# Attention with routed experts on one core: the merge of late batches, the gate and the first score are put at other places of a hand-written order

## The chip, the core and the metric

The kernel runs on one core of a Trainium2 chip. The metric is the device time of one execution in microseconds; three executions of the kernel before took 556.55 to 557.47 us, with a median of 557.07 us. The names of engines are those of the profile: PE is TensorE (matrix products, and transposes as products with an identity), PEld its weight loads, DVE is VectorE, ACT is ScalarE, POOL is GpSimd, SP is SyncE, which here only issues transfers.

## The reference

```python
batch, n_heads, seq, head_dim = (8, 12, 448, 64)
q_n, k_n = (rmsnorm(q, g_q), rmsnorm(k, g_k))
scores = scale * np.matmul(q_n, k_n.transpose(0, 1, 3, 2))
attn = softmax(scores)
x = matmul(attn, v)                 # as [3584 tokens, 768]
...
logits = x @ w_gate                 # 8 experts, w_gate [768, 8]
expert_idx = argmax(logits); gate_w = softmax(logits)[expert_idx]
for e in range(8):
    tok_idx = the tokens of expert e, at most the 80 with the largest gate_w
    h = maximum(x[tok_idx] @ w1[e], 0)      # [768, 1024]
    out[tok_idx] = gate_w[tok_idx] * (h @ w2[e])
```

So the attention of all 8 batches has to be done before it is known which 80 tokens each expert takes.

## The kernel before, in words

**Attention.** The 8 batches of 12 heads are cut into 24 groups `g` of 4 heads, three to a batch. A group has 7 rounds: six tiles of 128 keys (2 pairs of heads by 3) and one round with the 64 keys that are left of all four heads. A round is a score (L302: PE writes two banks of PSUM, ACT takes the exponential into an `at` tile) and, later, the product with V (`av`, L323). `presum` (L346, on DVE) adds the `at` tiles of a pair of heads, and `zl` (L366, on PE) brings those sums and the product of the attention output with the gate's weights into one bank. Ahead of its first score a group needs `square` (ACT), `rstd` (DVE; a power on POOL), `normalise` (POOL; DVE for the first two groups) and four `transp` (L281): (a, u) with a = 0 for q and 1 for k, and u for the pair of heads. Each `transp` is three or four PE transposes into the one bank `tp`, which ACT copies into `qkT`.

**Order.** Nothing is scheduled by a planner: the loop at L830 goes over slots `s`, two rounds each, 84 slots with attention work, and each engine runs its instructions in the order in which the loop emits them. A slot emits, one after another: the list `begins`; two scores; two presums; the list `mid`; one step of the hidden chains; two `av`; the list `end`; another step of the chains; then `work`, which emits rounds of the top-80 search on DVE as long as a credit lasts. `at_slot` (L766) fills the lists: b0 is the slot of a group's first score, and the table at L768 says what goes to which slot.

**Routing, hidden under the attention.** When a batch's third group is through, its gate follows: `gate1` (ACT copies the bank), `gate1t` (four PE transposes `zt`), `gate1v`, `gate2`, `gate2i` and `gate2b` (DVE; gate weights `gw` and the one-hot `eq`). For batches 0 to 3 the top 80 of each expert are searched together: `queue` holds ten rounds on 448 columns, `lists`, then ten rounds on 320 columns; `numbers` (L505, in `queue2`) fetches the token numbers through a table in DRAM and sets `first`. Batches 4 to 6 are then merged in, one after another, by two lists of steps: `ranks` (L541: p1/v1 and p2/v2, the rank of each token in its batch) and `merges` (L597: p0 transposes `eq`, L607; p1 compares with the list, L615; p2 counts, L635; p3 writes the new list with `put` and `keep`, L663 and L666; p4 transposes it, L674). The first number of a step is its lag in half slots behind the step before; `chain_step` (L741) emits a step when its lag is over and what it needs is there. Steps left over when the attention ends are emitted one after another behind it.

**End.** Batch 7 is ranked and merged in the open (L865 to L884) between runs of idle products that only keep PE busy (`busy`, L860), then eight experts run one after another (L926), with rows gathered by POOL (`gather`, L896). The weights of experts 3 to 7 were staged in DRAM before (`stage_w`), and those of experts 3 to 5 are loaded by SP (`fetch_late`, L176) into memory that the attention's tiles gave free, behind the last write of an attention output (`xout`, L685, on PE and ACT, then SP) to DRAM.

Of the kernel before, what the change touches and what calls it, by code (L numbers as in the profile page):

```python
# [20 lines left out]
def kernel(  # L21
# [13 lines left out]
    nc = tc.nc  # L35
# [44 lines left out]
    def load_g():  # L80
        for half in range(2):
            nc.scalar.dma_start(out=gk2[half * D:(half + 1) * D, 0:1], in_=g_q[:, None])
            nc.scalar.dma_start(out=gk2[half * D:(half + 1) * D, 1:2], in_=g_k[:, None])
# [106 lines left out]
    with tc.tile_pool(name="qk", bufs=4) as qkpool, \  # L190
# [302 lines left out]
        def lists(val, idx):  # L493


            def go():
                num = tpool.tile([128, CAP], U32, tag="own", name="num")
                nc.gpsimd.tensor_scalar(num[:, :], idx[:, :], offq[:, :], None, op0=ALU.add)
                for g in range(NB0):
                    c = slice(g * CAP, (g + 1) * CAP)  # L500
                    nc.sync.dma_start(out=tab_dram[:, c], in_=num[32 * g:32 * g + E, :])
                    nc.gpsimd.tensor_copy(canda[:, c], val[32 * g:32 * g + E, :])
            return [(0.0, go), (0.0, lambda: listed.append(True))]

        def numbers(idx):  # L505
# [29 lines left out]
            for e in range(E):  # L535
                todo.append((0.0, lambda e=e: fetch(e)))
                if e % 3 == 2:
                    todo.append(stop)
            return todo + [stop, stop, (0.3, close)]

        def rank_in_batch(b, hidden):  # L541
# [53 lines left out]
            return [(0, p1, v1, 4.6), (6, p2, v2, 0.4)]  # L595

        def merge(b, hidden):  # L597
# [84 lines left out]
            return [(0, p0, None, 0), (1, p1, v1, 1.0), (4, p2, v23, 1.7), (4, p3, None, 0),  # L682
# [26 lines left out]
        first, listed, queue, queue2 = [], [], [], []  # L709
# [31 lines left out]
        def chain_step(h, which, todo, brisk):  # L741
# [5 lines left out]
            if which == "r" and not listed:  # L747
                return False
# [19 lines left out]
        for g in range(NG):  # L768
# [3 lines left out]
            for a in range(2):  # L772
                if g == 0:
                    for x in range(2):
                        t = -10 + 4 * x
                        at_slot(mid, t, square, g, a, HALF[x])
                        at_slot(mid, t + 1, rstd, g, a, HALF[x])
                        at_slot(mid, t + 2, normalise, g, a, HALF[x])
                        if (a, x) != (1, 1):
                            at_slot(end, t + 2, transp, g, a, x)  # L780
                    continue
# [3 lines left out]
            if g:  # L785
                at_slot(end, b0 - 3, transp, g, 0, 0)
                at_slot(end, b0 - 2, transp, g, 1, 0)
                at_slot(end, b0 - 1, transp, g, 0, 1)
            at_slot(mid, b0, transp, g, 1, 1)
            at_slot(mid, b0 + 5, xout, g, 0)  # L790
            at_slot(mid, b0 + 6, xout, g, 1)
            at_slot(end, b0 + 4, zl, g)
            if g % NQ == NQ - 1:
                b = g // NQ
                at_slot(mid, b0 + 5, gate1, b)
                at_slot(end, b0 + 5, gate1t, b)
                at_slot(begins, b0 + 6, gate1v, b)
                if b == B - 1:
                    continue
                at_slot(begins, b0 + 6, gate2, b)  # L800
                at_slot(end, b0 + 6, gate2x, b)
                at_slot(end, b0 + 6, spent, 2.8)
                at_slot(end, b0 + 7, spent, 1.0)
                if b >= NB0:
                    at_slot(begins, b0 + 7, gate2i, b)
                at_slot(begins, b0 + 7, gate2b, b)
                if b == NB0 - 1:
                    at_slot(mid, b0 + 8, gate3)
                    at_slot(end, b0 + 8, queue.extend, topk)
                elif b >= NB0:  # L810
                    at_slot(begins, b0 + 7, batch_in, b)
# [18 lines left out]
        for s in range(-10, NS + 30):  # L830
# [10 lines left out]
            if not chain_step(2 * s, "m", merges, s > NS):  # L841
# [7 lines left out]
            work(2.0 if s < NS else 9)  # L849
# [147 lines left out]
```

## Time and profile before

| | |
|---|---|
| median of three executions | 557.07 us |
| the profiled execution's own time | 559.87 us |
| its span | 557.98 us (granted PE clock 0.946 of full on the mean) |
| PE busy | 516.2 us, 93% of the span |
| DVE, ACT, POOL busy | 336.0, 315.8, 286.0 us |

The profiled execution took 559.87 us, of which 557.98 are the span from its first to its last instruction. A busy PE does not mean that it works at full clock: the granted clock stands beside the busy time in the window view, 1.00 for 2.4 GHz and 0.50 for 1.2 GHz. In a timeline row, the number in brackets is the time that the engine stood idle before, with what ended it.

### The profile page before, as it was taken

What the parts mean: (1) busy time and instruction counts of PE and PEld (TensorE: products, weight loads), DVE (VectorE), ACT (ScalarE), POOL (GpSimd) and SP (SyncE); (2) the same over time, 40 slices, a digit from 0 to 9 for tenths busy, and PEclk for the clock granted to TensorE, in tenths of its full rate; (3) what the DMA queues carried; (4) which work ended last, traced back from release to release, by engine and by line L of the source; (5) the groups of instructions that cost most, each with busy time, mean ns of one, the idle gap of its engine ahead of it and who ended that gap; (6) DMA issues with size and microseconds to landing.
All of it is one profiled execution on the core that took longest, in us unless ns stands there. A gap on an engine that the chain in (4) does not pass through costs nothing. (4 is left out here: it accounts for less than half of the span.)

```text
span 558.0 us, 9382 instructions
## 1 busy us (share of the span) xinstructions
PE 516.2 (93%) x3499; PEld 243.9 (44%) x3499; DVE 336.0 (60%) x592; ACT 315.8 (57%) x527; POOL 286.0 (51%) x208
## 2 busy tenths in 40 slices
PE   7699999999999999999989979999999997689786
PEld 7234343334333433343324424334443346678664
DVE  3585545646746654399898496795766442343442
ACT  4776767777677776775747736746765541101111
POOL 1596593847747569267473764644776001003131
PEclk9799999999999999999989989989999995579999
DMA  5469959898697959958793976659679114936931
GB/s 165 132 119 224 269 143 198 211 226 184 179 209 222 182 165 233 208 169 179 206 215 98 200 205 121 187 136 222 150 146 196 34 34 152 430 133 191 386 110 54
DMA packets 107532, 100.74 MB, mean 181 GB/s; under 512 B 29152, under 2 KB 99296, under 8 KB 106208
## 3 DMA queue, kind: packets, MB, share of 16 engines
q1 hardware_dynamic: 90256, 70.74, 41.9%
q0 software_dynamic: 15872, 29.14, 29.6%
q8 instruction: 27, 0.44, 0.3%
q10 hardware_dynamic: 1360, 0.29, 0.2%
q14 instruction: 17, 0.14, 0.1%
HBM read 101.12 MB, written 39.91 MB: 253 GB/s over the span
## 5 line engine op out<-in xcount | busy, mean ns | idle before, releaser
L261 POOL TENSOR_TENSOR rs<-ms,nhalf 128x14 f32<-128x14 f32 (+1 forms) x48 | 144.4, 3012 | 156.2 <-DVE ms L254 141.8
L320 ACT ACTIVATE at<-ps 128x896 f32<-128x896 f32 x144 | 125.7, 915 | 36.4 <-PE ps L318 19.8
L318 PE MATMUL ps<-qkT 64*128 64x448 f32 x576 | 132.8, 573 | 0.0
L340 PE MATMUL po<-at,vt 128*64 128x448 f32 x576 | 128.0, 559 | 0.0
L253 DVE TENSOR_REDUCE ms<-sq 128x14 f32<-128x896 f32 (+2 forms) x52 | 52.6, 1012 | 83.6 <-ACT sq L244 79.8
L318 PEld LDWEIGHTS ps<-qkT 64*128 64x128 f32 x576 | 49.2, 188 | 50.6 <-issue 42.4
L272 POOL TENSOR_TENSOR qn<-qk,rs 128x768 f32<-128x768 f32 x44 | 70.8, 1608 | 0.2
L298 ACT ACTIVATE qkT<-tp,gqk 128x448 f32<-128x448 f32 (+2 forms) x72 | 34.0, 506 | 62.4 <-PE tp L290 51.2
L352 DVE TENSOR_TENSOR sm<-at 128x896 f32<-128x896 f32 x48 | 54.0, 1124 | 20.3 <-ACT at L320 20.3
L285 PEld LDWEIGHTS tp<-ident,qn 128*128 128x128 f32 x288 | 30.9, 144 | 69.0 <-issue 50.2
L285 PE MATMUL tp<-ident,qn 128*128 128x128 f32 x288 | 53.4, 296 | 6.6 <-DVE qn L272 5.5
L340 PEld LDWEIGHTS po<-at,vt 128*64 128x64 f32 x576 | 34.2, 136 | 55.1 <-issue 54.2
L359 DVE TENSOR_TENSOR sm<-sm,at 128x896 f32<-128x896 f32 x48 | 54.4, 1134 | 2.5 <-ACT at L320 1.2
L244 ACT ACTIVATE sq<-qk 128x896 f32<-128x896 f32 (+2 forms) x52 | 46.7, 905 | 4.4 <-DMA gk<-in_g_q_dram 4.2
L300 ACT COPY qkT<-tp 128x448 f32<-128x448 f32 (+2 forms) x72 | 27.2, 412 | 23.4 <-PE tp L290 21.0
L356 DVE TENSOR_TENSOR sm<-sm,ar 64x896 f32<-64x896 f32 x24 | 32.5, 1354 | 4.8 <-ACT ar L320 4.2
L373 PE MATMUL zl<-sm,zsel 128*32 128x448 f32 x192 | 28.4, 551 | 6.8 <-DVE sm L359 6.6
L938 ACT ACTIVATE h_sb<-ph 128x320 bf16<-128x320 f32 x16 | 6.9, 437 | 49.0 <-PE ph L934 46.9
L691 PEld LDWEIGHTS xp<-ident,us 128*128 128x128 f32 x192 | 20.5, 142 | 31.3 <-issue 29.2
L363 ACT COPY us<-po 128x448 f32<-128x448 f32 x48 | 25.7, 534 | 14.2 <-PE po L333 11.4
L691 PE MATMUL xp<-ident,us 128*128 128x128 f32 x192 | 31.9, 289 | 0.6 <-ACT qkT L300 0.6
L695 ACT COPY xb<-xp 128x512 f32<-128x512 f32 x48 | 28.2, 587 | 2.7 <-DMA xr_scratch<-xb 1.4
(155 smaller groups left out, 586.6 us busy)
## 6 DMA issues: line engine op xcount, KB each, us to landing
wb_scratch<-in_moe_w_dram POOLq DMA_DIRECT2D x10, 1536.0 KB
w_sb<-wb_scratch SPq DMA_DIRECT2D x10, 1536.0 KB
out_dram<-zeros SPq DMA_DIRECT2D x28, 384.0 KB
vt<-in_v_dram SPq DMA_DIRECT2D x24, 384.0 KB
w_sb<-in_moe_w_dram POOLq DMA_DIRECT2D x6, 1536.0 KB
xr_scratch<-xb SPq DMA_DIRECT2D x24, 384.0 KB
qk<-in_q_dram SPq DMA_DIRECT2D x23, 384.0 KB
qk<-in_k_dram SPq DMA_DIRECT2D x23, 384.0 KB
```

Of the source, the lines that this page charges most:

```text
L244: nc.scalar.activation(st[g]["sq%d" % a][:, lo:hi], st[g]["qk"][a][:, lo:hi], AF.Square)
L253: nc.vector.reduce_sum(out=ms[:, lo:hi], in_=st[g]["sq%d" % a][:, lo:hi], axis=AX.X)
L261: nc.gpsimd.tensor_tensor(rs[:, lo:hi], ms[:, lo:hi], nhalf[:, lo:hi], op=ALU.pow)
L272: eng.tensor_mul(qn[:, :M].rearrange("p (j h) d -> p h j d", h=4)[:, h0:h1], qk[:, h0 * NJ:h1 * NJ].rearrange("p (h j) d -> p h j d", j=NJ ...
L285: nc.tensor.transpose(tp[:, j * 128:(j + 1) * 128], qn[:, 4 * j + 2 * u:4 * j + 2 * u + 2].rearrange("p h d -> p (h d)"), ident[:, :])
L298: nc.scalar.activation(o, x, AF.Copy, scale=gqk[:, :])
L318: nc.tensor.matmul(ps[:, hh, :S], T1[d, u, j * 128:(j + 1) * 128], T0[d, u, :], start=True, stop=True)
L320: nc.scalar.activation(at[:], ps[:, :, :S], AF.Exp)
L340: nc.tensor.matmul(st[g]["po%d" % u][hh * D:(hh + 1) * D, :S], vt[:, (2 * u + hh) * NJ + j, :], at[:, hh, :], start=(x == 0), stop=(x == R ...
L352: nc.vector.tensor_add(sm[:], s["at%d" % (x - 1)][:], s["at%d" % x][:])
L359: nc.vector.tensor_add(sm[:], sm[:], s["at%d" % x][:])
L691: nc.tensor.transpose(xp[:, j * 128:(j + 1) * 128], us[:, c:c + 128], ident[:, :])
```

## The change

`load_g` issues the four small loads of the gains from POOL and not from ACT. Group 0's transposes for the second pair of heads go behind the first slot's scores, and group 1's move with them. `zl` is emitted a slot later, the gate steps one to two slots later and behind the presums and not ahead of them (`mid` and not `begins`), with `gate2i`, `gate3`, `batch_in` and the credit that they take (`spent`). `ranks` wait until the whole search of the first list is emitted (`queue` empty) where they waited for its first half (`listed`). The fetches of `numbers` go four to a slot and not three. The lags of p2 and p3 in `merges` are 3 and not 4, that of p2 in `ranks` 5 and not 6, and the credit for search rounds is 2.15 per slot and not 2.0.

```diff
@@ load_g
-            nc.scalar.dma_start(out=gk2[half * D:(half + 1) * D, 0:1], in_=g_q[:, None])
-            nc.scalar.dma_start(out=gk2[half * D:(half + 1) * D, 1:2], in_=g_k[:, None])
+            nc.gpsimd.dma_start(out=gk2[half * D:(half + 1) * D, 0:1], in_=g_q[:, None])
+            nc.gpsimd.dma_start(out=gk2[half * D:(half + 1) * D, 1:2], in_=g_k[:, None])
@@ lists, numbers
-            return [(0.0, go), (0.0, lambda: listed.append(True))]
+            return [(0.0, go)]
-                if e % 3 == 2:
+                if e % 4 == 3:
                     todo.append(stop)
-            return todo + [stop, stop, (0.3, close)]
+            return todo + [stop, (0.3, close)]
@@ rank_in_batch, merge
-            return [(0, p1, v1, 4.6), (6, p2, v2, 0.4)]
+            return [(0, p1, v1, 4.6), (5, p2, v2, 0.4)]
-            return [(0, p0, None, 0), (1, p1, v1, 1.0), (4, p2, v23, 1.7), (4, p3, None, 0),
+            return [(0, p0, None, 0), (1, p1, v1, 1.0), (3, p2, v23, 1.7), (3, p3, None, 0),
                     (1, p4, None, 0)]
@@ chain_step
-            if which == "r" and not listed:
+            if which == "r" and queue:
                 return False
@@ the table of slots
-                        if (a, x) != (1, 1):
-                            at_slot(end, t + 2, transp, g, a, x)
+                    at_slot(end, -8, transp, g, a, 0)
+                    at_slot((end, mid)[a], a, transp, g, a, 1)
                     continue
...
-                at_slot(end, b0 - 3, transp, g, 0, 0)
-                at_slot(end, b0 - 2, transp, g, 1, 0)
+                at_slot(end, b0 - 3 + (g == 1), transp, g, 0, 0)
+                at_slot((end, mid)[g == 1], b0 - 2 + (g == 1), transp, g, 1, 0)
                 at_slot(end, b0 - 1, transp, g, 0, 1)
-            at_slot(mid, b0, transp, g, 1, 1)
+                at_slot(mid, b0, transp, g, 1, 1)
...
-            at_slot(end, b0 + 4, zl, g)
+            at_slot(end, b0 + 5, zl, g)
...
-                at_slot(mid, b0 + 5, gate1, b)
-                at_slot(end, b0 + 5, gate1t, b)
-                at_slot(begins, b0 + 6, gate1v, b)
+                at_slot(mid, b0 + 6, gate1, b)
+                at_slot(end, b0 + 6, gate1t, b)
+                at_slot(mid, b0 + 7, gate1v, b)
...
-                at_slot(begins, b0 + 6, gate2, b)
-                at_slot(end, b0 + 6, gate2x, b)
+                at_slot(mid, b0 + 8, gate2, b)
+                at_slot(end, b0 + 8, gate2x, b)
...
-                at_slot(begins, b0 + 7, gate2b, b)
+                at_slot(mid, b0 + 9, gate2b, b)
@@ the loop over slots
-            if not chain_step(2 * s, "m", merges, s > NS):
+            if s < NS + 2 and not chain_step(2 * s, "m", merges, s > NS):
                 chain_step(2 * s, "r", ranks, s > NS)
...
-            work(2.0 if s < NS else 9)
+            work(2.15 if s < NS else 9)
```

What this does to the order is seen at three places. The first is PE at its start, behind the idle products `wps` that open the program: `tp` is a transpose, `ps` a score, `po` the product with V. Before:

```order
L285 MATMUL tp<-ident,qn 128x128 x3
L290 MATMUL tp<-ident,qn 128x128
L285 MATMUL tp<-ident,qn 128x128 x3
L290 MATMUL tp<-ident,qn 128x128
L285 MATMUL tp<-ident,qn 128x128 x3
L318 MATMUL ps<-qkT 128x448 x4
L285 MATMUL tp<-ident,qn 128x128 x6
L290 MATMUL tp<-ident,qn 128x128
L318 MATMUL ps<-qkT 128x448 x2
L311 MATMUL ps<-qkT 64x448 x4
L340 MATMUL po<-at,vt 64x448 x4
```

and now:

```order
L285 MATMUL tp<-ident,qn 128x128 x3
L290 MATMUL tp<-ident,qn 128x128
L285 MATMUL tp<-ident,qn 128x128 x3
L290 MATMUL tp<-ident,qn 128x128
L318 MATMUL ps<-qkT 128x448 x4
L285 MATMUL tp<-ident,qn 128x128 x3
L318 MATMUL ps<-qkT 128x448 x2
L311 MATMUL ps<-qkT 64x448 x4
L285 MATMUL tp<-ident,qn 128x128 x3
L340 MATMUL po<-at,vt 64x448 x4
L285 MATMUL tp<-ident,qn 128x128 x3
L290 MATMUL tp<-ident,qn 128x128
```

The first two scores no longer stand behind the third transpose; group 1's first transpose (the one with an L290 behind it) moved from ahead of the second pair of scores to behind the first product with V.

The second place is PE behind a batch's last group, here the first batch's (`zl` are L373 and L377, `zt` the gate's transposes, `xp` those of `xout`). Before:

```order
L318 MATMUL ps<-qkT 128x448 x4
L340 MATMUL po<-at,vt 64x448 x4
L373 MATMUL zl<-sm,zsel 32x448 x4
L377 MATMUL zl<-us,wgs 32x448 x4
L285 MATMUL tp<-ident,qn 128x128 x3
L290 MATMUL tp<-ident,qn 128x128
L311 MATMUL ps<-qkT 64x448 x4
L318 MATMUL ps<-qkT 128x448 x2
L691 MATMUL xp<-ident,us 128x128 x4
L340 MATMUL po<-at,vt 64x448 x4
L387 MATMUL zt<-ident,zsb 128x128 x4
```

and now:

```order
L318 MATMUL ps<-qkT 128x448 x4
L340 MATMUL po<-at,vt 64x448 x4
L285 MATMUL tp<-ident,qn 128x128 x3
L290 MATMUL tp<-ident,qn 128x128
L311 MATMUL ps<-qkT 64x448 x4
L318 MATMUL ps<-qkT 128x448 x2
L691 MATMUL xp<-ident,us 128x128 x4
L340 MATMUL po<-at,vt 64x448 x4
L373 MATMUL zl<-sm,zsel 32x448 x4
L377 MATMUL zl<-us,wgs 32x448 x4
```

`zl` has a whole slot more of PE work ahead of it than the presums that it reads; `zt` stands a slot later too.

The third place is PE around the last product with V (L340). Before, the following comes behind it: the end of batch 4's merge and the start of batch 5's,

```order
L691 MATMUL xp<-ident,us 128x128 x4
L663 MATMUL mp<-info,put 80x16 x4
L666 MATMUL mp<-ainfo,keep 80x2 x8
L387 MATMUL zt<-ident,zsb 128x128 x4
L674 MATMUL mp<-ident,ainfo 8x80
L691 MATMUL xp<-ident,us 128x128 x4
L607 MATMUL mp<-ident,eq 8x128 x4
L615 MATMUL mp<-aval,eqT 128x80 x4
```

and a few rows on the end of batch 5's merge and the start of batch 6's:

```order
L663 MATMUL mp<-info,put 80x16 x4
L666 MATMUL mp<-ainfo,keep 80x2 x8
L674 MATMUL mp<-ident,ainfo 8x80
L607 MATMUL mp<-ident,eq 8x128 x4
L615 MATMUL mp<-aval,eqT 128x80 x4
```

Now batch 5's merge ends ahead of the last product with V, and only batch 6's stands behind it, with `zl` between its steps:

```order
L663 MATMUL mp<-info,put 80x16 x4
L666 MATMUL mp<-ainfo,keep 80x2 x8
L674 MATMUL mp<-ident,ainfo 8x80
L340 MATMUL po<-at,vt 64x448 x4
L607 MATMUL mp<-ident,eq 8x128 x4
L691 MATMUL xp<-ident,us 128x128 x4
L615 MATMUL mp<-aval,eqT 128x80 x4
L373 MATMUL zl<-sm,zsel 32x448 x4
L377 MATMUL zl<-us,wgs 32x448 x4
```

Batch 4's p0 stands behind the scores of the 83rd slot in the old order, and behind those of the 76th in the new one.

## Rows read from the trace of the kernel before

**Rows 1.** Window view: span, busy us (instructions) of PE, PEld, DVE, ACT, POOL, PEclk, DMA

```profile
0.00:456.00 456.00, 436.78 (x2588) 177.57 (x2590) 299.46 (x506) 302.01 (x492) 267.90 (x189) 0.98 0.76 176
456.00:486.30 30.30, 20.93 (x139) 17.23 (x136) 8.92 (x26) 5.72 (x16) 2.12 (x3) 0.57 0.60 240
```

**Rows 2.** Timeline of PE: start us, us, engine, line, op, out<-in [idle before]; three stalls

```profile
288.88 0.57 PE L373 MATMUL zl<-sm,zsel 128*32 128x448 f32 x2 [2.54 <-DVE sm L359]
...
329.78 0.57 PE L373 MATMUL zl<-sm,zsel 128*32 128x448 f32 x2 [3.34 <-DVE sm L359]
...
364.08 0.71 PE L552 MATMUL mp<-ident,rg 128*128 128x128 f32 x4 [2.72 <-DVE rg L435]
```

**Rows 3.** Window view, as rows 1, of the stretch behind the first stall

```profile
290.00:293.00 3.00, 3.00 (x12) 1.02 (x12) 2.93 (x7) 0.63 (x2) 2.89 (x2) 0.50 1.10 233
```

**Rows 4.** Timeline of PE around the end of the attention and up to the experts

```profile
446.91 0.60 PE L607 MATMUL mp<-ident,eq 128*8 128x128 f32 x4
...
449.09 1.11 PE L615 MATMUL mp<-aval,eqT 8*128 8x80 f32 x8
...
453.34 2.48 PE L340 MATMUL po<-at,vt 128*64 128x448 f32 x12
...
457.71 0.32 PE L635 MATMUL mp<-eqb,ahead 128*80 128x8 bf16 x4
...
459.83 0.78 PE L663 MATMUL mp<-info,put 128*80 128x16 f32 x8 [1.31 <-DVE put L653]
...
463.61 1.06 PE L691 MATMUL xp<-ident,us 128*128 128x128 f32 x4
...
475.25 0.30 PE L674 MATMUL mp<-ident,ainfo 80*8 80x80 f32 x1 [0.31 <-ACT ainfo L670]
...
486.33 4.47 PE L863 MATMUL hot<-identb 128*128 128x128 bf16 x40
...
500.47 1.51 PE L666 MATMUL mp<-ainfo,keep 80*80 80x1 f32 x16
...
508.49 1.88 PE L934 MATMUL ph<-xgT,w_sb 128*128 128x80 bf16 x48 [0.50 <-DVE xgT L920]
```

**Rows 5.** Timeline of PE at the start of the program

```profile
18.05 0.87 PE L285 MATMUL tp<-ident,qn 128*128 128x128 f32 x3 [4.09 <-DVE qn L272]
...
24.22 0.53 PE L285 MATMUL tp<-ident,qn 128*128 128x128 f32 x3 [1.18 <-DVE qn L272]
...
24.79 1.02 PE L318 MATMUL ps<-qkT 64*128 64x448 f32 x4
```

**Rows 6.** Timeline of ACT at the start

```profile
7.09 1.33 ACT L244 ACTIVATE sq<-qk 128x384 f32<-128x384 f32 x4 [4.24 <-DMA gk<-in_g_q_dram]
...
23.45 0.95 ACT L244 ACTIVATE sq<-qk 128x896 f32<-128x896 f32 x1
```

**Rows 7.** Timeline of SP's transfers: the rest of group 2's load of q

```profile
18.40 1.25 SPq L214 DMA_DIRECT2D qk<-in_q_dram  x2
```

**Rows 8.** Timeline of POOL: its first transfer of the program

```profile
35.75 1.09 POOL L162 DMA_DIRECT2D w_sb<-in_moe_w_dram  x1
```

**Rows 9.** Timeline of SP at the end: the weights of experts 3 to 7

```profile
468.86 49.25 SPq L176 DMA_DIRECT2D w_sb<-wb_scratch  x10
```

**Rows 10.** Window view, as rows 1, of that load and behind it

```profile
468.00:492.00 24.00, 16.06 (x115) 14.25 (x114) 6.67 (x19) 3.30 (x11) 2.12 (x3) 0.52 0.93 384
492.00:496.00 4.00, 3.82 (x39) 3.51 (x40) 2.64 (x8) 0.39 (x2) 0.00 (x0) 0.82 0.21 64
```

**Rows 11.** Timeline of POOL: the first gather, and the fifth

```profile
502.97 0.98 POOL L900 DMA_INDIRECT xg<-xr_scratch,idxT  x1 [31.96 <-DVE idxT L887]
...
515.87 0.98 POOL L900 DMA_INDIRECT xg<-xr_scratch,idxT  x1 [0.30 <-issue]
```

**Rows 12.** Timeline of DVE: the first reader of each of these two gathers

```profile
506.59 0.95 DVE L909 TENSOR_TENSOR xn<-xg 80x768 bf16<-80x768 f32 x1 [4.41 <-DMA xg<-xr_scratch,idxT]
...
526.46 0.95 DVE L909 TENSOR_TENSOR xn<-xg 80x768 bf16<-80x768 f32 x1 [3.49 <-DMA xg<-xr_scratch,idxT]
```

More of the change, by code (lines that the diff above doesn't have):

```diff
@@ L708 @@
         v03 = tpool.tile([128, CAP], F32, name="v03")
-        first, listed, queue, queue2 = [], [], [], []
+        first, queue, queue2 = [], [], []
         r, ix = rounds(lambda: gst[0]["R"], 128, S, v03)
@@ L785 @@
             if g:
-                at_slot(end, b0 - 3, transp, g, 0, 0)
-                at_slot(end, b0 - 2, transp, g, 1, 0)
+                at_slot(end, b0 - 3 + (g == 1), transp, g, 0, 0)
+                at_slot((end, mid)[g == 1], b0 - 2 + (g == 1), transp, g, 1, 0)
                 at_slot(end, b0 - 1, transp, g, 0, 1)
-            at_slot(mid, b0, transp, g, 1, 1)
+                at_slot(mid, b0, transp, g, 1, 1)
             at_slot(mid, b0 + 5, xout, g, 0)
             at_slot(mid, b0 + 6, xout, g, 1)
-            at_slot(end, b0 + 4, zl, g)
+            at_slot(end, b0 + 5, zl, g)
             if g % NQ == NQ - 1:
                 b = g // NQ
-                at_slot(mid, b0 + 5, gate1, b)
-                at_slot(end, b0 + 5, gate1t, b)
-                at_slot(begins, b0 + 6, gate1v, b)
+                at_slot(mid, b0 + 6, gate1, b)
+                at_slot(end, b0 + 6, gate1t, b)
+                at_slot(mid, b0 + 7, gate1v, b)
+                at_slot(end, b0 + 7, spent, 1.3)
                 if b == B - 1:
                     continue
-                at_slot(begins, b0 + 6, gate2, b)
-                at_slot(end, b0 + 6, gate2x, b)
-                at_slot(end, b0 + 6, spent, 2.8)
-                at_slot(end, b0 + 7, spent, 1.0)
+                at_slot(mid, b0 + 8, gate2, b)
+                at_slot(end, b0 + 8, gate2x, b)
+                at_slot(end, b0 + 8, spent, 1.5)
                 if b >= NB0:
-                    at_slot(begins, b0 + 7, gate2i, b)
-                at_slot(begins, b0 + 7, gate2b, b)
+                    at_slot(mid, b0 + 9, gate2i, b)
+                at_slot(mid, b0 + 9, gate2b, b)
+                at_slot(end, b0 + 9, spent, 1.0)
                 if b == NB0 - 1:
-                    at_slot(mid, b0 + 8, gate3)
-                    at_slot(end, b0 + 8, queue.extend, topk)
+                    at_slot(end, b0 + 9, gate3)
+                    at_slot(end, b0 + 9, queue.extend, topk)
                 elif b >= NB0:
-                    at_slot(begins, b0 + 7, batch_in, b)
+                    at_slot(mid, b0 + 9, batch_in, b)
         at_slot(begins, 0, load_wgs)
```

## The prediction

> **What bounds the kernel now.** I read the stages first, then who makes PE wait, then the end of the program in order of time. In the window view [rows 1] the attention fills the first 456 us, and PE is busy in 436.8 of them: in this stage the time is PE's work plus PE's stalls. The 30 us behind it are another matter: PE is busy in 20.9 of 30.3 us at a mean clock of 0.57, on a chain of small products, each of which waits for ACT or DVE and hands on to them. The reader should see in the timeline [rows 4] what this chain is: the last product with V starts at 453.34 and ends at 455.82, then come the end of batch 4's merge, all of batch 5's and all of batch 6's, and only at 486.33 the idle products that open batch 7's. So 30.5 us of the program are merges that found no place under the attention.
>
> The stalls [rows 2] are few and long: PE stands for 2.54 and 3.34 us before a `zl` that reads presums not yet done on DVE, and for 2.72 us before a transpose of gate weights that DVE delivers late. Behind the first of them the window [rows 3] has PE busy all the time at a granted clock of 0.50, that is 1.2 GHz, with DVE busy in 2.93 of 3.00 us. The same view shows the same behind the other two, each time for at least the 3.0 us of such a window and, between neighbours at 1.00, for at most 4.5; I take 3.4.
>
> All sums below stand against the profiled execution, 559.87 us (span 557.98). It is 2.8 us above the median of the runs; I take the differences over to the median.
>
> **The start: -2.0 us.** PE waits 4.09 us for the third transpose's input and 1.18 us for group 1's [rows 5]; the first scores need neither, so at most 5.3 us are to be had. They are not all had. In ACT's order the square of group 2's q stands ahead of the copy that the slot's fourth score needs. Its load is issued until 19.65 [rows 7], in the buffer that group 0's q leaves free, and the square ran at 23.45 without an idle time before it [rows 6]: the load landed between the two, and I take 21.5. With the square (0.95) and a copy (0.6) the fourth score starts at 23.0, with 1.4 us of transposes (two of 0.53, and 0.3 for the short fourth product of one) still to do that were done by then in the old order; there it started at 25.8 (24.79 and one score of 1.02 [rows 5]). That leaves 1.4 us. The loads of the gains leave ACT too: ACT stood 4.24 us before its first squares, and what ended that was the last of these loads in its own stream [rows 6], so the squares can start earlier, by 2 us at the most if the data is there. On POOL four such transfers take 4 x 1.09 us [rows 8], not much less than ACT lost, and DVE multiplies the gains before it normalises: I take 0.6. Bounds of the part: +1.0 (gains late) and -4.6.
>
> What speaks against that last move is a rule of the Trainium skill (DMA: Bandwidth & Descriptors, Specifications): a simple load belongs on SP or ACT, where the first byte takes about 0.6 us against about 1 us from GpSimd. By that rule the gains would land 0.4 us later and the start would be worth 1.6 us; rows 6 show against it that the loads held up the squares on ACT, and no row here shows the first byte of such a load from POOL.
>
> **The stalls: -12.2 us.** `zl` goes a slot later. A slot is 5.2 us (84 of them lie between 18.9 and 455.8 [rows 4, 5]), more than the longest of these waits, so both `zl` waits fit into the delay. The rank's transpose that waited 2.72 us comes, for batches 4 and 5, behind the whole search, when its gate weights are long there. Gone are 2.54 + 3.34 + 2.72 = 8.6 us [rows 2], and with the stalls the stretches at half clock behind them: 3 x 3.4 us, in which half the work is lost, 5.1 us [rows 3]. New waits: batch 6's rank now follows its gate weights within the slot, and the copies between p0 and p1 and between p3 and p4 stand close; 1.5 us for them. The gate work on DVE costs nothing more behind the presums: DVE has 299.5 us of work in 456, and less waiting, since `gate1v` no longer stands ahead of presums that are ready. Bounds: -13.7, and -2 if DVE stays the pace (a rival).
>
> **Merges under the attention: +7.5 us.** PE has no free time there once the stalls are gone, so their work counts in full, at full clock [rows 4]: p0 0.60, p1 1.11, p2 0.32, p3 0.78 + 1.51, p4 0.30, which is 4.6 us for batch 5 and 2.9 us for the p2 to p4 of batch 4. ACT's and DVE's shares of a merge (about 2 us each) lie beside PE. The fetches, four to a slot, stand in POOL's queue beside `normalise` of the last two groups; POOL is busy in 267.9 of 456 us [rows 1], and these transposes come two slots behind, so I cost them at nothing. If that cover fails, a transpose waits, and the time is a stall as above.
>
> **Behind the attention: -20.5 us.** Call T' the end of the last product with V. Then only batch 6's merge is left, with `zl` and `xout` between its steps: p0 0.6, a transpose of `xout` 0.5 (half of the 1.06 at 463.61, at half clock), p1 1.1, `zl` 1.9 (455.82 to 457.71), from p2 to p3 2.1 (457.71 to 459.83, which takes in `xout` and `zt`), p3 2.1, then 0.31 + 0.30 for p4 [rows 4]: 8.9, and 1.1 for the copy of `eqT` and a share at half clock makes 10.0. Before it was 30.5. Bounds: 9 and 11.
>
> **The first gathers: +4.6 us.** Here something is late next. The weights of experts 3 to 5 start at 468.86 [rows 9], 5.25 us behind the last `xout` on PE (463.61), and end near 492.6 [rows 10], 23.7 us later. Both ends now shift with T': `xout` at T' + 4.4, weights from T' + 9.6 to T' + 33.3. The first gather was issued by 503.95, 17.6 us behind the idle products' start, so now by T' + 27.6, into the last 6 us of that load, which took a DMA share of 0.93 and 384 GB/s. Undisturbed a gather landed in 2.64 us (503.95 to 506.59); the fifth, issued by 516.85 beside weights of experts 6 and 7, took 9.6 us, until 526.46 [rows 11, 12]. I let the first gather land 1 us behind the weights, T' + 34.3 in place of T' + 30.2, 4.1 us late, and add 0.5 us for products at half clock behind that idle time. Bounds: nothing, and 7.0 + 1.7 = 8.7. The experts keep their 49 us; their own weights come as before, relative to them.
>
> **Sum:** -2.0 - 12.2 + 7.5 - 20.5 + 4.6 = **-22.6 us**, 537.3 us for the profiled execution and **534.5 us** at the median.
>
> **Rivals.**
> *The gathers slip between the weights.* Then the 4.6 us are not paid: 529.9 us. For it: the gather is small beside what is left of the load. Against it: the 9.6 us of the fifth. The Trainium skill (DMA: Bandwidth & Descriptors, SWDGE vs HWDGE vs iDMA) has each DMA engine go round its queues in turn, so a gather would share and not wait; the fifth gather speaks against that here. Chance 0.20.
> *DVE stays the pace.* The new credit emits more search rounds to a slot, and DVE had 2.93 of 3.00 us busy behind a stall [rows 3]; the lag then outgrows the slot that `zl` was given, other stalls take the old ones' place, and the stalls' part is worth 2 us: 544.7 us. Against it: over the attention DVE has a third of its time free. Chance 0.18.
> *Slower: merge steps as stalls.* Eight merge steps (p2 to p4 of batch 4, p0 to p4 of batch 5) now stand in PE's order ahead of scores. Should each wait for ACT or DVE as long as the worst stall, 3.34 us, and drop the clock for 1.7 more [rows 2, 3], that is 40.3 us on top, 574.8 us; it decides from five of the eight on (22.6 / 5.04). Against it: p0 and p1 of batch 4 [rows 4] ran under the attention without a wait. Chance 0.03.
> *The change doesn't do what it says:* the order has the merges ahead of the last product with V whatever runs late, so only the start could fail to move; that is inside the range.
>
> **How the numbers follow.** The forecast has a chance of 0.56, its own range 529 to 540. The three rivals have 0.41, and 0.03 is left for gains lost in a way I don't see, up to no change. Range: down to the first rival with the start at its best, 527, up to the second, 545; outside it stay the slower rival, the rest, and the ends of several bounds at once. A measurement tells 0.2%, 1.1 us, from no change. Faster by more than that 0.95, within it 0.01, slower 0.04.
>
> **What would show it.** In the new profile: p0 of batch 4 near 397 us (seven slots of 5.2 and the 14 us of the first two parts before 446.9), and one merge behind the last product with V, 9 to 11 us before the idle products; no stall over 1 us at `zl` and a clock of 1.00 from 30 to 440 us; the end of the last product with V near 449 (455.8 - 2.0 - 12.2 + 7.5); the first score some 4 us before the third transpose's old place at 18.05; `xn` waiting 7 to 10 us for the first gather. It is wrong if a stall of 2 us or more stands at another line inside the attention, if T' comes later than 453, or if the first gather lands within 3 us.

## Result and the profile after

The changed kernel takes **537.47 us** (median of four runs, 536.77 to 544.34) against 556.81 us for the kernel before in the same rounds: ratio 0.9685, 95% interval 0.9603 to 0.9767. Timed once more beside later experiments it took 535.62 us (six runs, 533.81 to 537.20), ratio 0.9616 (0.9586 to 0.9646). The forecast was 534.5 us, range 527 to 545. Its profiled execution took 536.96 us with a span of 535.1 us, 22.9 us less than the one of before (forecast: 22.6 less). Between these two executions the sum was right to 0.3 us; between the medians the change is worth 19.3 us, 21.4 the second time. The terms of the sum were not right.

The windows of the changed kernel that answer to [rows 1], and one inside the attention (the last three columns are PE's granted clock, DMA share, GB/s):

```profile
0.00:448.00 448.00, 433.58 (x2661) 180.31 (x2662) 306.65 (x514) 303.92 (x500) 269.23 (x193) 0.99 0.78 180
448.00:457.00 9.00, 7.29 (x73) 5.43 (x72) 5.03 (x16) 3.49 (x10) 0.55 (x1) 0.91 0.16 51
404.00:407.00 3.00, 2.90 (x11) 2.12 (x13) 2.96 (x4) 1.06 (x3) 0.00 (x0) 0.54 1.00 139
```

Where 30 us at a clock of 0.57 stood, 9 us at 0.91 are left. The end of the attention on PE, to be read against [rows 4]:

```profile
445.83 1.72 PE L340 MATMUL po<-at,vt 128*64 128x448 f32 x8
447.48 0.60 PE L607 MATMUL mp<-ident,eq 128*8 128x128 f32 x4
...
448.80 1.11 PE L615 MATMUL mp<-aval,eqT 8*128 8x80 f32 x8 [0.28 <-ACT eqT L610]
...
451.49 0.32 PE L635 MATMUL mp<-eqb,ahead 128*80 128x8 bf16 x4
...
453.41 0.66 PE L387 MATMUL zt<-ident,zsb 128*128 128x128 f32 x4 [1.11 <-ACT zsb L382]
453.90 0.68 PE L663 MATMUL mp<-info,put 128*80 128x16 f32 x8
...
456.17 0.30 PE L674 MATMUL mp<-ident,ainfo 80*8 80x80 f32 x1 [0.31 <-ACT ainfo L670]
456.26 3.63 PE L864 MATMUL hot<-identb 128*128 128x128 bf16 x40
```

The last product with V ends at 447.55, 8.3 us earlier than before, and one merge is left: the idle products follow 8.7 us later, where they followed 30.5 us later. But the experts begin at 485.96, which is 29.7 us behind the idle products (before: 486.33 to 508.49, 22.2 us), and then take 49.1 us (before 49.5). So the four stretches give -8.3, -21.8, +7.5 and -0.4: -22.9 us.

The -8.3 us is a balance too. The start of one slot's first score in both traces, changed kernel first, then before, in pairs:

```profile
52.50 0.65 PE L318 MATMUL ps<-qkT 64*128 64x448 f32 x2
...
359.40 0.65 PE L318 MATMUL ps<-qkT 64*128 64x448 f32 x2
```

```profile
52.71 0.65 PE L318 MATMUL ps<-qkT 64*128 64x448 f32 x2
...
378.37 0.65 PE L318 MATMUL ps<-qkT 64*128 64x448 f32 x2
```

At 52 us the change is 0.2 us ahead, at 359 us 19.0, and at T' 8.3. The start gave almost nothing, the stalls 18.8 us (12.2 forecast), and the last 90 us gave 10.7 of that back: the eight merge steps, which read start to start take 6.2 us of PE (7.5 forecast), and a new wait.

```profile
404.10 1.04 PE L387 MATMUL zt<-ident,zsb 128*128 128x128 f32 x4 [2.81 <-ACT zsb L382]
```

It is the longest wait of PE behind the start of the changed attention, and the window from 404 to 407 above shows the half clock behind it. ACT is late because DVE's `presum` is, and DVE stood in `close`, which ends the search of the first list; DVE, then POOL:

```profile
397.88 3.22 DVE L531 TENSOR_TENSOR ainfo<-num,bad 80x8 f32<-80x8 uint32 x1 [5.14 <-DMA num<-tab_scratch,add]
```

```profile
388.99 1.81 POOL L523 DMA_INDIRECT num<-tab_scratch,add  x1 [0.30 <-issue]
...
397.82 1.46 POOL L272 TENSOR_TENSOR qn<-qk,rs 128x768 f32<-128x768 f32 x1
399.25 0.39 POOL L278 TENSOR_TENSOR qn<-qk,rs 128x128 f32<-128x128 f32 x1
399.61 1.46 POOL L272 TENSOR_TENSOR qn<-qk,rs 128x768 f32<-128x768 f32 x1
401.04 1.31 POOL L278 TENSOR_TENSOR qn<-qk,rs 128x128 f32<-128x128 f32 x1
```

Two other waits take the place of old ones. At the start, on ACT and behind it on PE:

```profile
22.52 0.95 ACT L244 ACTIVATE sq<-qk 128x896 f32<-128x896 f32 x1 [3.64 <-DMA qk<-in_q_dram]
23.38 0.56 ACT L298 ACTIVATE qkT<-tp,gqk 128x384 f32<-128x384 f32 x1
```

```profile
14.38 1.77 PE L318 MATMUL ps<-qkT 64*128 64x448 f32 x8 [0.62 <-ACT qkT L300]
...
23.99 0.97 PE L311 MATMUL ps<-qkT 64*64 64x448 f32 x4 [3.78 <-ACT qkT L298]
```

And ahead of the experts, on POOL and on DVE:

```profile
479.68 1.04 POOL L901 DMA_INDIRECT xg<-xr_scratch,idxT  x1 [21.08 <-DMA xr_scratch<-rg]
```

```profile
483.87 0.95 DVE L910 TENSOR_TENSOR xn<-xg 80x768 bf16<-80x768 f32 x1 [11.81 <-DMA xg<-xr_scratch,idxT]
```

The gather doesn't wait for its indices, which were there at 471.9, but for batch 7's gate rows, which ACT wrote with two transfers (19.5 and 3.2 KB) issued by 461.8, under the weights' load (SP, from 456.45). In the kernel before, ACT issued them from 491.57 to 493.48, when that load was about over [rows 10].

### The profile page after: what moved, and what is told of

It is laid out like the page before. It is cut to its first block, busy times and chain, and to the rows that moved or that the text cites. A ratio compares the mean times of both kernels' runs of the same rounds, so it can differ in the third digit from the quotient of the medians.

```text
span 535.1 us, 9378 instructions
## 1 busy us (share of the span) xinstructions
PE 499.0 (93%) x3499; PEld 235.0 (44%) x3499; DVE 339.5 (63%) x592; ACT 315.2 (59%) x527; POOL 287.1 (54%) x212
## 5 line engine op out<-in xcount | busy, mean ns | idle before, releaser
L340 PE MATMUL po<-at,vt 128*64 128x448 f32 x576 | 128.3, 560 | 0.0
L352 DVE TENSOR_TENSOR sm<-at 128x896 f32<-128x896 f32 x48 | 58.8, 1224 | 26.2 <-ACT at L320 26.2
L285 PEld LDWEIGHTS tp<-ident,qn 128*128 128x128 f32 x288 | 30.5, 142 | 65.7 <-issue 55.7
L340 PEld LDWEIGHTS po<-at,vt 128*64 128x64 f32 x576 | 34.1, 137 | 54.4 <-issue 53.3
L363 ACT COPY us<-po 128x448 f32<-128x448 f32 x48 | 25.9, 539 | 12.2 <-PE po L333 9.9
L895 POOL MEMSET xg<- 80x781 f32 x3 | 2.2, 755 | 53.2 <-DVE lmax L413 53.2
L354 DVE TENSOR_TENSOR sm<-sm,ar 64x896 f32<-64x896 f32 x24 | 28.4, 1182 | 0.8
## 6 DMA issues: line engine op xcount, KB each, us to landing
w_sb<-wb_scratch SPq DMA_DIRECT2D x10, 1536.0 KB, 13.2
```

Of the source, the lines that this page charges most:

```text
L285: nc.tensor.transpose(tp[:, j * 128:(j + 1) * 128], qn[:, 4 * j + 2 * u:4 * j + 2 * u + 2].rearrange("p h d -> p (h d)"), ident[:, :])
L340: nc.tensor.matmul(st[g]["po%d" % u][hh * D:(hh + 1) * D, :S], vt[:, (2 * u + hh) * NJ + j, :], at[:, hh, :], start=(x == 0), stop=(x == R ...
L352: nc.vector.tensor_add(sm[:], s["at%d" % (x - 1)][:], s["at%d" % x][:])
```

## The experiments

Each of the single edits starts from the changed kernel, so each is to be held against its 535.6 to 537.5 us and against its trace. Ratios are to the kernel before, in the same rounds.

**Gate rows ahead of the weights.** SP writes them, and then loads.

```diff
-            eng = nc.sync if b < B - 1 else nc.scalar
+            eng = nc.sync
...
         load_weights(wlate, e, e)
-        fetch_late(e)
...
     gate2b(b)
+    for e in range(NW0, NW0 + 3):
+        fetch_late(e)
```

> The changed kernel with one edit: batch 7's gate rows are written to DRAM by SP ahead of the loads of the weights of experts 3 to 5 (before: by ACT, while those loads run). In the changed kernel the first gather is issued at 479.7, 7.8 us after its indices (471.9), and the profile has it wait for that write. Theory A (the small writes are what the load holds up, the gather itself is quick): the rows land about 462, the gather is issued about 473 and lands in 3 to 5 us though the load runs until about 485; experts from 478 in place of 486.0, time about 530. Theory B (what the prediction said: the load holds up the gather itself): the gather is issued at 473 and lands 1 us behind the load, about 486; no gain, 536 to 539.

533.54 us (two runs), ratio 0.955 (0.9447 to 0.9654). POOL issues the gather as soon as the indices are there, 6.4 us earlier, and `xn` now waits for the gather itself:

```profile
473.23 1.04 POOL L902 DMA_INDIRECT xg<-xr_scratch,idxT  x1 [14.11 <-DVE idxT L889]
```

```profile
481.64 0.95 DVE L911 TENSOR_TENSOR xn<-xg 80x768 bf16<-80x768 f32 x1 [9.22 <-DMA xg<-xr_scratch,idxT]
```

It takes 8.4 us from issue to `xn`, beside the load (the window from 472 to 482 us has the DMA engines full), and the experts begin 26.9 us behind the idle products, not 29.7. Between the two theories: the gate rows cost 2.8 us, and under them lies the slow gather that the prediction had priced, 26.9 - 22.2 = 4.7 us.

**Two experts' weights behind the gathers, by POOL.**

```diff
         load_weights(wlate, e, e)
-        fetch_late(e)
+        if e == NW0:
+            fetch_late(e)
...
     for e in range(3):
         gather(e)
+    for e in range(NW0 + 1, NW0 + 3):
+        fetch_late(e, nc.gpsimd)
```

> The changed kernel, with only expert 3's weights loaded ahead of the gathers, those of experts 4 and 5 issued by POOL behind the first three gathers. Both theories have the rows of batch 7 written by about 467, the first gather issued at 473 and landed at about 476, and the experts start at about 478 in place of 486.0. They differ behind that: A (small writes suffer, gathers hardly) keeps the experts' stage at 49 us, time about 529; B (a gather beside a load takes 7 us more) makes the gathers of experts 3 to 5 late, with stalls of 3 us each before two or three experts, time about 534.

542.27 us (two runs), ratio 0.9707 (0.9592 to 0.9821), slower than either theory had it. The first half came true: the first gather lands 3.8 us after its issue (471.27 to 475.10), and the experts begin 22.4 us behind the idle products, as in the kernel before. Then the fourth gather, issued on POOL behind the weights:

```profile
474.84 2.25 POOL L176 DMA_DIRECT2D w_sb<-wb_scratch  x4
477.40 1.37 POOL L902 DMA_INDIRECT xg<-xr_scratch,idxT  x1 [0.30 <-issue]
```

```profile
507.50 0.95 DVE L911 TENSOR_TENSOR xn<-xg 80x768 bf16<-80x768 f32 x1 [20.51 <-DMA xg<-xr_scratch,idxT]
```

30 us from issue to `xn`.

**The same weights, issued by ACT** behind expert 0's two relu steps, to tell whether POOL's queue or the late weights did this.

```diff
         load_weights(wlate, e, e)
-        fetch_late(e)
+        if e < NW0 + 1:
+            fetch_late(e)
...
                                  ph[:], AF.Relu)
+            if e == 0 and NW0 + 1 + fh < NW0 + 3:
+                fetch_late(NW0 + 1 + fh, nc.scalar)
```

> Only expert 3's weights are loaded ahead of the gathers; those of experts 4 and 5 are issued by ACT, each behind one of expert 0's two relu steps, and no longer by POOL as in the run before. Theory A: in that run the fourth gather was 20.5 us late because it stood behind the weights in POOL's own queue, not because the weights came too late. Then no gather keeps `xn` waiting over 5 us, the experts begin 22 to 24 us behind the idle products that open batch 7's rank (29.7 in the changed kernel), and the time is about 530. Theory B: whatever load is moved behind the gathers, the experts then wait for weights; a wait of 10 us or more stands before one of the experts 3 to 5, and the time is 540 or more.

543.09 us (two runs), ratio 0.9733 (0.9631 to 0.9835). Both theories hold in part: the experts begin 22.2 us behind the idle products, as theory A had it, and the time is that of theory B, though PE's only wait for weights is 2.0 us. The fourth gather landed 3.4 us after its issue, but ACT issued its loads just behind it (from 482.35), so it says nothing of POOL's queue. The next three, beside these loads, landed 13.2, 11.5 and 12.0 us after their issue; in the run before, the fourth and the fifth took 30.1 and 27.4. So a load on another queue makes these gathers late too, and one on POOL's own queue cost some 15 us more. The three late gathers keep `xn` waiting 6.1, 2.7 and 4.8 us, and the stage of the experts takes 62.3 us and not 49.1. The windows say why:

```profile
467.00:480.00 13.00, 11.34 (x148) 11.07 (x146) 6.04 (x17) 0.00 (x0) 2.96 (x3) 0.75 0.22 54
480.00:525.00 45.00, 28.96 (x412) 23.04 (x413) 15.04 (x31) 5.24 (x12) 9.13 (x9) 0.88 0.90 336
```

Ahead of the gathers the DMA engines stand at a share of 0.22 for 13 us, where the changed kernel has 0.92 from 456 to 482; the weights of experts 4 to 7 then fill them for 45 us. The early load is slow for the gathers, and pays.

**The gains' product later**, behind `normalise`.

```diff
-        at_slot(end, -9, gains)
+        at_slot(mid, -8, gains)
```

> The changed kernel, with the product of the two gains emitted on DVE behind group 0's first normalise and not ahead of it. In the changed kernel DVE waits 2.2 us there for the gains' loads from POOL (they land at about 10.5). Theory A (that wait holds up the whole start): the first transpose moves from 11.5 to about 9.3, the first score from 14.4 to about 12.5, the load of group 2's q goes out 2 us earlier, and slot 2's scores start at about 27.2 in place of 29.2; time 2 us less. Theory B (behind it the data of groups 1 and 2 set the pace): first score at 12.5, but slot 2 still at 29 and no gain.

536.52 us (two runs), ratio 0.9604 (0.9499 to 0.9708). DVE no longer stands before `gains` while `normalise` could run, but the gains themselves still come at 10.6 us, and PE's first idle products end only at 11.8 (10.7 in the changed kernel); the first score starts at 14.55, 0.2 us later. So most of the 2.2 us that DVE waited there were not on the path: in the changed kernel PE waited 0.84 us behind them, before the first transpose, and here the idle products fill that time.

**Group 2's squares a slot later.**

```diff
-                at_slot(mid, b0 - 7 + a, square, g, a)
-                at_slot(end, b0 - 7 + a, rstd, g, a)
+                at_slot(mid, b0 - 7 + a + (g == 2), square, g, a)
+                at_slot(end, b0 - 7 + a + (g == 2), rstd, g, a)
```

> The changed kernel, with group 2's squares and their sums one slot later, so that on ACT the first of them no longer stands ahead of the copy that the fourth score needs. Theory A (that square, waiting 3.6 us for its load, is what stops PE for 3.8 us): the fourth score comes at about 20 in place of 24.0, no half clock follows, and slot 2 starts at about 25.5 in place of 29.2; time 3 to 4 us less. Theory B (group 1's data are as late: its transpose at 28.5 waits for DVE at 23.8 and for the bank): slot 2 at 27.5 or later, 1 to 2 us less, or nothing if group 2's sums come late to POOL.

530.81 us (two runs, 527.0 and 534.62), ratio 0.9502 (0.931 to 0.9693). The wait of 3.78 us on PE is gone and the third slot begins early:

```profile
24.30 0.65 PE L318 MATMUL ps<-qkT 64*128 64x448 f32 x2
```

In the changed kernel that score starts at 29.22. From the next slot on every start is 4.7 us earlier, unchanged until 350 us. That is what the new start had to give; ACT's square on late data had kept it. The time is less clear: the two runs lie 7.6 us apart, and the profiled one, the slower, ends 2.4 us ahead of the changed kernel.

**The last staging behind the fetches.**

```diff
-            at_slot(begins, 2 + 5 * (2 * e + i),
+            at_slot(begins, 2 + 5 * (2 * e + i) + (4 if (e, i) == (E - 1, 0) else 0),
```

> Only one transfer moves: POOL's staging of the last expert's first matrix (1536 KB, issue to landing 14 us) is issued four slots later, behind all eight fetches of the first list's numbers and not between the fourth and the fifth. Theory A, the queue: fetches 5 to 8, issued at 385.3 to 389.0, all landed between 397.1 and 397.6, just behind the staging that was issued at 382.4 and landed at 397.0, so they stood behind it in POOL's queue. Then the numbers are there by about 392, DVE's wait before `ainfo` falls from 5.1 us to under 1, the gate's transposes no longer wait 2.8 us, and the time falls by 2.8 + 1.7 us to about 532.5. Theory B, the fetches are slow by themselves, or ACT and DVE are late there for other work: the wait stays over 3 us and the time within 1 us of 537.

535.22 us (two runs), ratio 0.9592 (0.953 to 0.9654). The DMA issues from 385 to 390 us (median us to landing last), changed kernel, then experiment:

```profile
num<-tab_scratch,add POOLq DMA_INDIRECT x4, 10.2
```

```profile
num<-tab_scratch,add POOLq DMA_INDIRECT x4, 2.3
```

And in the experiment `close` runs without a wait:

```profile
392.71 0.17 DVE L531 TENSOR_TENSOR ainfo<-num,bad 80x8 f32<-80x8 uint32 x1
```

So the staging had made the fetches late. That they stood behind it in POOL's queue, and did not merely share busy DMA engines with it (share 0.88 from 383 to 397 us), is borne out by the fourth fetch of the changed kernel: issued just ahead of the staging, it landed after 4.5 us. PE's wait for `zsb` is gone, with the half clock. The time tells less, since the changed kernel has that wait only in some executions: in a second profile of it, taken with the last runs, `close` waits even longer, yet its addition then takes 0.32 us and not 3.22, and POOL's next step takes 1.32 us where it took 0.39:

```profile
398.37 0.32 DVE L531 TENSOR_TENSOR ainfo<-num,bad 80x8 f32<-80x8 uint32 x1 [6.26 <-DMA num<-tab_scratch,add]
```

```profile
397.20 1.46 POOL L272 TENSOR_TENSOR qn<-qk,rs 128x768 f32<-128x768 f32 x1
398.63 1.32 POOL L278 TENSOR_TENSOR qn<-qk,rs 128x128 f32<-128x128 f32 x1
```

PE's wait for `zsb` is 0.38 us there. Between 397 and 411 us that profile gains 4.1 us on the first, with no edit at all: the price of the stall. So late fetches alone did not stop PE; the stall came where the long addition followed them.

**Old slots for `zl` and the gate.** The lines of the table from `zl` to `batch_in` are those of the kernel before, the merges stay changed.

> The changed kernel with `zl`, the gate steps, gate3, batch_in and the credit they take back in the slots of the kernel before; merges, ranks, fetches and the start stay changed. Theory A, the trace comparison: the waits at `zl` cost more than PE's idle rows showed, 16 us or more over the attention, since many of them were covered by the modelled tails of matmuls; then the end of the last product with V comes at 560 - 112 + 12 to 16, that is 12 to 16 us later than in the changed kernel (447.6), and the time is 549 to 553. Theory B, the prediction's sizes: two waits of 2.5 and 3.3 us with 1.7 us of half clock each, 9.3 us: about 546. Theory C: the waits came from the merges and fetches of the old order, not from the slots: within 2 us of 537.

571.44 us (two runs), ratio 1.0241 (1.0152 to 1.0331): slower than the kernel before, and outside all three theories. T' comes at 475.5 us, 28 us later than in the changed kernel. PE's waits at `zl`:

```profile
271.25 0.96 PE L373 MATMUL zl<-sm,zsel 128*32 128x448 f32 x2 [2.73 <-DVE sm L359]
294.90 0.96 PE L373 MATMUL zl<-sm,zsel 128*32 128x448 f32 x2 [2.52 <-DVE sm L359]
335.98 0.96 PE L373 MATMUL zl<-sm,zsel 128*32 128x448 f32 x2 [4.07 <-DVE sm L359]
417.61 0.87 PE L373 MATMUL zl<-sm,zsel 128*32 128x448 f32 x2 [3.70 <-DVE sm L359]
```

Against the changed kernel the starts around the first three fall back by 5.2, 5.5 and 6.6 us, so a wait costs what its row shows and 2.4 to 3.0 us more. Another 3.7 us are lost ahead of the first, the rest behind the third. The direction of the first theory holds, not its size: with the new merges the late `zl` and gate, which this edit moved together, are worth 28 us at T', more than everything that the old order lost to waits. Why it is that much was not taken apart.

**Old merges, ranks and fetches**, with the new start, `zl` and gate.

```diff
-            return [(0.0, go)]
+            return [(0.0, go), (0.0, lambda: listed.append(True))]
...
-            if which == "r" and queue:
+            if which == "r" and not listed:
```

and the old lags, stops and credit, and no bound on a slot's first chain step.

> The changed kernel with ranks, lags, fetches, credit and the second chain step as in the kernel before, so that two merges stand behind the last product with V again; `zl`, the gate and the start stay changed. Theory A, the prediction's terms for these parts: 20.5 us come back behind the attention, 7.5 us leave the attention, 4.6 us leave the gathers: 537.0 + 8.4 = 545.4. Theory B, the sizes read from the changed trace: 21.8 come back, 5.8 of merge steps and 4.5 of the stall behind the first list's numbers leave, 7.5 leave the gathers: 541. Theory C, the merges lay in PE's gaps and cost nothing under the attention: 21.8 come back and only 7.5 leave, 551.

544.69 us (two runs), ratio 0.9762 (0.9714 to 0.981), nearest to the prediction's own terms. T' comes at 443.8 us, 3.8 us before that of the changed kernel; the idle products follow 29.3 us behind it (473.05) and not 8.7, and the experts 23.1 us behind those and not 29.7. With the rank ahead of the search its wait is back, which [rows 2] had shown:

```profile
361.40 1.17 PE L552 MATMUL mp<-ident,rg 128*128 128x128 f32 x4 [4.45 <-DVE rg L435]
```

So ranks behind the search cure a stall of their own, which the second theory had left out.

**Three together:** the gate rows first, the squares a slot later and the staging behind the fetches.

> Three of the single edits together on the changed kernel: group 2's squares a slot later, the last staging behind the fetches, batch 7's gate rows written ahead of the weights. Theory A, the three lie one behind another on the path and add up: 4.7 us at the start, 4.5 us behind the first list's numbers, 2.8 us from the idle products of batch 7's rank to the experts (26.9 us there in place of 29.7): 537.0 - 12.0 = 525.0. Theory B, one of them only moves the wait (the weights' load of 40 us for five experts, or DVE, is the pace): 529 or more.

526.86 us (six runs, 525.23 to 529.96), ratio 0.9451 (0.9416 to 0.9487). The changed kernel itself, in the same rounds:

> The changed kernel itself, for a comparison on the same chip and in the same rounds as the two runs before: 537 by either theory.

535.62 us. The three take 8.8 us off (1.6%) and beat both kernels; 12.0 was expected if each counted in full. In its profile the start is 4.7 us earlier, no PE wait inside the attention is over 1.5 us, and the experts begin 27.7 us behind the idle products, 2.0 less. Those two make 6.7; the staging can only save its 4.1 us in the executions that have the stall.

**Two experts ahead, not three**, on top of these.

```diff
-    for e in range(NW0, NW0 + 3):
+    for e in range(NW0, NW0 + 2):
         fetch_late(e)
...
+            if e == 0 and NW0 + 2 + fh < NW0 + 3:
+                fetch_late(NW0 + 2 + fh, nc.scalar)
```

> The run before with one more edit: the weights of expert 5 are issued by ACT behind expert 0's first relu, so that two experts' weights and not three are loaded ahead of the gathers. Theory A, only the load that runs while the gathers are out costs: they land within 4 us of their issue, the experts begin 23.5 us behind the idle products, and the time is 3.4 us under that of the run before, 521.6. Theory B, a load that is pushed behind the gathers meets the later gathers (two experts' weights pushed back cost 13 us of the experts' stage in the run with ACT): half of that, 6.5, less 3.4: 3 us over the run before, 528.

529.66 us (six runs, 526.87 to 532.07), ratio 0.9499 (0.9462 to 0.9537): 2.8 us over the run before, as theory B had it, though the ranges of the two overlap. The experts begin 1.9 us sooner behind the idle products (25.8 us), but their stage takes 54.9 us and not 49.2: later gathers keep `xn` waiting longer, up to 5.1 us.

## Why the prediction was right, and where it wasn't

**Behind the attention** (-20.5): -21.8, right in mechanism and near in size. Batch 6's merge alone is left, in 8.7 us (10.0 forecast); the run with the old merges puts 20.6 us back.

**Merges under the attention** (+7.5): 6.2 us of PE. The steps cost their products and hardly a wait (0.26 us, once); the durations of [rows 4] overlap with those of their neighbours, and start to start a step is shorter (p0 0.53, p3 1.74 and 2.14 us).

**The stalls** (-12.2): -18.8, less 4.1 for the new one. The mechanism was right and the term too small, in three places. One: the price of a `zl` wait. Between the starts of scores around the two of [rows 2] the change gains 5.5 and 5.8 us, 2.5 to 2.9 over PE's idle row, and the experiment with the old slots shows the same surcharge. The half clock was sized right: a mean of 0.57 over 4.00 us, between neighbours at 1.00, is 3.4 us at 0.50, 1.7 us lost.

```profile
289.50:293.50 4.00, 4.00 (x20) 1.14 (x14) 3.86 (x9) 0.84 (x2) 3.39 (x2) 0.57 1.11 244
```

The rest is mostly wait that PE's row doesn't show, since it counts from the modelled end of the product before. PE's weight loads stood 0.8 us longer at the same two places:

```profile
288.88 0.11 PEld L373 LDWEIGHTS zl<-sm,zsel 128*32 128x32 f32 x2 [3.34 <-DVE sm L359]
...
329.78 0.11 PEld L373 LDWEIGHTS zl<-sm,zsel 128*32 128x32 f32 x2 [4.14 <-DVE sm L359]
```

Two: short waits were not counted. Another 3.1 us were gained before 279 us, where PE's idle rows show no more than 0.58 and 0.71 us. Of these 1.5 and 1.1 us were gained around two more waits of `zl`, which the weight loads show in the kernel before:

```profile
145.78 0.11 PEld L373 LDWEIGHTS zl<-sm,zsel 128*32 128x32 f32 x2 [1.38 <-DVE sm L359]
...
251.35 0.11 PEld L373 LDWEIGHTS zl<-sm,zsel 128*32 128x32 f32 x2 [0.93 <-DVE sm L359]
```

The first weight load of a `zl` stands 0.70 us in both kernels; in the changed one none stands longer. Three: the other 4.4 us, the rank's wait among them, stand with new waits already taken off (the longest 1.35 us, at 354.93); the prediction had 4.4 for the rank and took 1.5 off.

**The fetches ("I cost them at nothing")**: this step failed. POOL's time was looked at, its queue was not: the staging of 1536 KB was issued at 382.4 us between the fourth and the fifth fetch and landed at 397.0; the last four fetches landed at 397.1 to 397.6. With the staging behind the fetches the wait is gone. It stopped PE only where the addition in `close` then took about 3 us, in four of seven profiles; in the other three `close` waited as long, and PE had no wait of note at `zt`. The text said that "a stall of 2 us or more stands at another line inside the attention" would make it wrong, and one does, at `zt`.

**The start** (-2.0): -0.2. The step that failed is "I take 21.5" for the landing of group 2's q, and with it that PE's wait behind it was given no price. The square ran at 22.52 behind a wait of 3.64 us, so the fourth score came at 23.99 where 23.0 was forecast, after PE had stood 3.78 us; then the clock was 0.50 for 3.4 us, 1.7 us lost (the window from 25.5 to 28.5 us has 0.50). Of the 0.6 us taken for the gains' loads 0.2 came: the first transpose starts at 11.54 and not 11.74, since DVE waited for the gains until 10.58. The question left out was what else to move past the slot; one slot for the squares is worth 4.7 us.

**The first gathers** (+4.6): +7.5. The mechanism priced (a gather beside the load lands late) shows only with the gate rows first: 4.7 us there. In the changed kernel the step that failed is the gather's issue, forecast at T' + 27.6: it was out by T' + 33.2, behind the gate rows, when that load was nearly over, and `xn` ran 3.2 us later. The gate rows' write, which the prediction didn't look at, took 17.6 us beside that load, and writing it first saves 2.8 us. The rule of the Trainium skill that was weighed there (DMA: Bandwidth & Descriptors, SWDGE vs HWDGE vs iDMA: the engines go round their queues in turn) does not save a small transfer from waiting here: 3.2 KB on ACT's queue needed 17.6 us beside three experts' weights on SP's, and 5.2 us where one expert's were ahead (the run with ACT).

**The rivals.** Gathers that slip between the weights: no, beside the load the first gather took 8.4 us from issue to `xn` (gate rows first), against 3.6 in the kernel before. DVE as the pace: no, the stalls gave more than forecast. Merge steps as stalls: no, under the attention the longest wait at one is 0.26 us. But the run with the old gate slots, 571 us, shows that the new merges need the late `zl` and gate.

## What to carry to other kernels

A transfer that was small in bytes was late here where a large one stood ahead of it, on its own queue or beside it. So list what each queue holds at that moment, and not only how busy the issuing engine is. A wait of 2.5 to 4.1 us on PE cost 2.4 to 3.0 us beyond its idle row here, 1.7 of them by the half clock behind it; a short one can be missing from PE's rows and show at its weight loads. And when a sum comes out right, look at the terms: here it was luck, since stalls worth 6.6 us more than forecast, and 2.6 us less for the merges, paid for 4.1 us of new stall, 2.9 of gathers and 1.8 at the start.

## What was not expected of the hardware

An addition of 80x8 elements on DVE took 0.17 us (beside POOL's `rs` step, from 392.50), 0.32 us, and 3.22 us, from 397.88 to 401.10, which is when the third of POOL's `normalise` steps in a row had ended. In seven profiles with the staging between the fetches it took 2.99 to 3.44 us in four and 0.32 to 0.99 in three. The Trainium skill (SBUF — State Buffer, SBUF: two separate sides) says that DVE, when it reads two operands from SBUF, and GpSimd exclude each other, the first to start holding the port for its whole instruction. The long additions agree with that, but the one beside `rs` does not: POOL's `rs` reads two operands from SBUF too, takes 2.6 us, and did not hold it up. That DVE loses to three POOL instructions in a row, and not to one, is more than the page says. No run parted the two engines, so that the port is the reason is not shown.

In these runs POOL's transfers landed in the order of issue also where a small one followed a large one: 2.3 us from issue to landing with none ahead, 8.6 to 11.8 us behind 1536 KB, 27 to 30 us behind four such. Whether the gate rows' 17.6 us, on ACT's queue, come from the write or from the signal of its end was not tried.
